# Unread products of TensorE placed by the planner, and weight loads that wait for the one before the last

## The chip, the cores and the metric

The kernel runs on one core of one Trainium2 chip, in one launch. The metric is the device time of one execution in microseconds. The kernel before the change takes 1048.31 us (median of 3 runs, 1048.13 to 1048.65).

## What is computed

Chunked attention with memory keys, followed by two feed-forward layers over the same 3072 tokens:

```python
for c in range(nc):                       # 24 chunks of 32 queries, 16 keys to the left, 8 to the right, 8 memory keys
    scores = scale * np.matmul(q_c, k_full.transpose(0, 1, 3, 2))
    scores = scores - np.max(scores, axis=-1, keepdims=True)
    a = np.exp(scores)
    a = a / (np.sum(a, axis=-1, keepdims=True) + 1e-09)
    out[:, :, c_start:c_end] = np.matmul(a, v_full)
...
x = out.transpose(0, 2, 1, 3).reshape(3072, 512)
h = x @ w_in                              # 512 x 2048
x = (h * np.clip(h + 3.0, 0.0, 6.0) / 6.0) @ w_out
h = x @ w2_in
out = np.maximum(0.01 * h, h) @ w2_out
```

Four batches, 8 heads of 64, 768 tokens each. The four weight matrices come as 64-bit floats.

## The kernel before

Every matrix product of the layers is made of three products of TensorE: an operand is split into a high part that TensorE takes exactly and the low rest (`xh`, `xl`; the two halves of a `w` tile), and high by high, high by low and low by high are added up in PSUM. A weight block (128 by 512) is loaded as 512 KB of 64-bit words into a `w` tile and decoded: absolute value on ACT (line 397), clamp, shift, sign and low bits on DVE (lines 400, 404, 408, 412), then the high part (a cast on ACT, line 342) and the low part (a difference on DVE, line 345). The reference's two layers are worked off in blocks of 512 tokens; later blocks are paired and use seven products in place of eight (line 1327). That part makes up most of the run and is not touched.

The beginning is what the change is about. The first 512 tokens come from two units of attention of 384 tokens (heads 0 to 3 in PSUM pair `at`, heads 4 to 7 in pair `ab`) and two half units (in banks `h` and in pair `ac`). Each goes through the same steps: load of queries and keys, copies of key windows (line 342, on ACT, DVE or POOL), scores on PE (lines 549 and 816), maximum on DVE, exponentials on ACT (lines 573, 585, 842, 850), sum and normalisation on DVE (lines 603, 867), transposes on PE (607, 871), a copy on ACT, product with the values on PE (627, 887), and the split into `xh` (ACT) and `xl` (DVE, line 345). Then come the hidden products `h` of layer 1 (line 1003), the gate on ACT and DVE which gives `g`, and the output products `y` (line 1052).

Nothing of the order is written down by hand. Every step is a `Task` with a key, a cost for each engine that may do it, the steps it comes after, and the buffers that it takes (`allocs`) and uses. `schedule` plays through these with its own costs (among them a model of SP's loads and of the delivery of PE's instructions, `feed`) and issues the steps in the order in which they are picked; each engine then works through its queue in order. The chip waits on semaphores, so the planner's times only set the order.

TensorE is kept at work in the beginning by products whose result nobody reads, the identity by itself into pair `ac`:

```python
x = made(b)[:, 1, N - 128 * c:].rearrange("p (a n) -> p a n", a=c)
for _ in range(n):
    nc.tensor.matmul(x, ident, ident.unsqueeze(1).to_broadcast([128, c, 128]), ...)
```

`warm(n, after)` makes a step of n of them; the four calls after the half units and the loop behind them give their places: 6 of 512 columns and 12 of 256, each tied to a step after which it comes. The last twelve go to the very `ac` in which the second half unit's scores lie. A product of 32-bit numbers is two instructions of TensorE in the profile, so `x4` there is two products here.

SP issues all loads in the planner's order. `LOADS` and `WEIGHTS` are the keys of the first of them. A load waits for a free buffer and for one of eight slots; the first weight loads wait for nothing else.

Of the kernel before, what the change touches and what calls it, by code (L numbers as in the profile page):

```python
# [25 lines left out]
NC = G // CHUNK  # L26
# [31 lines left out]
RATE_QK, RATE, RATE_V, COLD = 380.0, 220.0, 300.0, 1.1  # L58
# [10 lines left out]
class Task:  # L69


    def __init__(self, fn, opts, key, after=(), allocs=(), uses=(), moe=False, issues=1, late=0, loads=False, ins=8):
        self.late, self.loads, self.ins = late, loads, ins
# [21 lines left out]
STARTS, LANDS, SURE = 1900.0, 500.0, 1500.0  # L95
HELD, FETCHED, FETCH, STALL = 447, 256, 5000.0, 250.0
# [7 lines left out]
def schedule(tasks, places, ends):  # L104
# [10 lines left out]
    queue = (0, HELD, None)  # L115

    def feed(at, task):
        used, held, comes = queue
        for _ in range(task.ins):
            if comes is not None and comes <= at:  # L120
                held, comes = held + FETCHED, None
            if comes is None and used >= held - FETCHED:
                comes = at + FETCH
# [35 lines left out]
    def finish(task, e):  # L159
        for b in task.bufs:  # L160
# [6 lines left out]
        for t in task.next:  # L167
# [3 lines left out]
            if not t.left:  # L171
                push(now + (MARGIN if "PE" in t.opts and not t.moe else 0.0), "ready", t)
# [5 lines left out]
    while events:  # L178
# [10 lines left out]
        while again:  # L189
            again = False  # L190
            for e, h in heaps.items():
# [32 lines left out]
                if pick is None:  # L224
                    continue
                pick.taken = True
                for b in pick.allocs:
# [8 lines left out]
                if e == "SP" or pick.loads:  # L236
                    at = now
                    for _ in range(pick.issues):
                        at = max(at, lanes[e].pop(0)) + ISSUE[e]
                        wire = max(wire, at + STARTS) + d / pick.issues  # L240
                        lanes[e].append(wire + LANDS)
                    free[e] = at if pick.loads else max(at, wire - QUEUED)
                    push(free[e], "free", None)
                    push(wire + LANDS + (SURE if pick.allocs else 0.0), "done", (pick, e))
# [12 lines left out]
def tile_attn_moe_moe2(ctx: ExitStack, tc: tile.TileContext, raw, w1i, w1o, w2i, w2o, out):  # L257
# [131 lines left out]
    def decode(src, f, key, early=None, after=(), place="wm", gate=(), late=0, own=True, split=None):  # L389
# [3 lines left out]
        def load(e):  # L393
            nc.sync.dma_start(out=make(t, ([128, 512, 2], U32)).rearrange("p w s -> p (w s)"), in_=src[f])
# [19 lines left out]
        k = add(load, {"SP": dma(524288, 380.0)}, key - 30 if early is None else early, after=after, allocs=[t])  # L414
# [31 lines left out]
    xbuf, xdone, turn, sent = {}, {}, [], {}  # L446

# [9 lines left out]
    marks = {}  # L457

    def warm(n, after=None, home=None):

        b, c = home or Buf("ac"), 2 if home else 4

        def fn(e):
            x = made(b)[:, 1, N - 128 * c:].rearrange("p (a n) -> p a n", a=c)
            for _ in range(n):
                nc.tensor.matmul(x, ident, ident.unsqueeze(1).to_broadcast([128, c, 128]), start=True, stop=True, skip_group_check=True)  # L466

        add(fn, {"PE": c * n * (220.0 if after else 430.0)}, after.key + 0.5 if after else -200.0, after=[after] if after else [], allocs=[] if home else [b], uses=[home] if home else [], ins=4 * n)

    def unit(j, quad, key, tag, own=False, direct=False, loads=None):  # L470
# [254 lines left out]
        t = marks["s", j, quad] = add(scores, {"PE": (COLD if direct else 1.0) * 1300.0}, key - 16, ins=192, after=t, allocs=[ps], uses=[*qk, *kw])  # L725
        scored = t
        if direct and quad in SHIFT:
            t = add(greatest, {"DVE": 2100.0}, key - 15, after=[t], allocs=[mx, e], uses=[ps])
            t = add(exp_all, {"ACT": act(2 * PAIRS * W)}, key - 13, after=[t], uses=[e])
            t = add(total, {"DVE": 1250.0}, key - 12, after=[t], allocs=[s], uses=[e])  # L730
        else:
# [4 lines left out]
            t = add(exp(1), {"ACT": 6 * 330.0}, key - 13, after=[t], uses=[ps, mx, e, s])  # L736
# [3 lines left out]
        t = add(take_p, {"ACT": act(PAIRS * 128)}, key - 5, after=[t], uses=[pt, e])  # L740
        t = marks["v", j, quad] = add(values_whole if plain else values, {"PE": (COLD if direct else 1.0) * 1600.0}, key, ins=192, after=[t, *l2], uses=[e, *v, ps])
# [12 lines left out]
    def half_unit(j, quad, gp, key, tag, loads, copies, cold):  # L754
# [195 lines left out]
        l1 = add(load_qk, {"SP": dma(128 * 2 * QK * 4, RATE_QK)}, loads[0], allocs=[qk])  # L950
# [4 lines left out]
        t = marks["s", j, quad, gp] = add(scores, {"PE": cold * 650.0}, key - 16, ins=96, after=[t], allocs=banks, uses=[qk, kw])  # L955
        marks["b", j, quad, gp] = banks
        if gp or quad not in SHIFT_HALF:
            t = add(greatest, {"DVE": 700.0}, key - 15, after=[t], allocs=[mx], uses=banks)
            t = add(exp, {"ACT": 6 * 330.0}, key - 13, after=[t], allocs=[e, s], uses=[*banks, mx])
            t = add(total, {"DVE": 350.0}, key - 12, after=[t], uses=[s])  # L960
        else:
            t = add(greatest, {"DVE": 1250.0}, key - 15, after=[t], allocs=[mx, e], uses=banks)
# [3 lines left out]
        t = marks["t", j, quad, gp] = add(transpose, {"PE": cold * 300.0}, key - 7, ins=6, after=[t], uses=[e, *banks])  # L966
        t = add(take_p, {"ACT": act(NC * 128)}, key - 5, after=[t], uses=[*banks, e])
        t = marks["v", j, quad, gp] = add(values_whole if whole else values, {"PE": cold * 900.0}, key, ins=96, after=[t, l2], uses=[e, v, *banks])
# [445 lines left out]
    def made_as(b, shape):  # L1414
        return b.t if b.t is not None else make(b, (shape, F32))
# [149 lines left out]
    warm(2)  # L1565
    warm(1, marks["s", 0, 0])
# [124 lines left out]
```

## Time and profile before

| | |
|---|---|
| median of 3 runs | 1048.31 us |
| profiled execution | 1049.14 us |
| its span | 1047.4 us |
| PE busy | 1035.1 us, 99% |
| DVE busy | 875.3 us, 84% |
| ACT busy | 693.7 us, 66% |
| POOL busy | 20.8 us, 2% |
| first hidden product of layer 1 | 39.77 us |

A timeline row gives the start, the time to the end of the last instruction in it, the engine, the line, the tiles and, in brackets, how long the engine had stood idle and what released it. Neighbouring rows overlap a little, as instructions are pipelined. In the stretches the granted clock is a mean: 1.00 is full speed, 0.50 half.

### The profile page before, as it was taken

The numbers are of one execution on the slowest core, as the hardware profiler recorded it, in microseconds if no ns is written. First come the engines' busy times: TensorE is split into PE (matmuls) and PEld (weight loads), VectorE is DVE, ScalarE is ACT, GpSimd is POOL, SyncE is SP. The second block draws the span as 40 slices with busy tenths as digits, with TensorE's granted clock in tenths as the row PEclk, the third lists the DMA queues.
The fourth block names the chain that finished last, engine by engine and source line by source line (L and its number), as shares of the span: only waits on it lengthen the run. The fifth ranks groups of instructions, "written<-read, shape, count | busy, mean of one in ns | idle before, by whom it ended". The sixth has DMA issues, their size and how long they took to land.

```text
span 1047.4 us, 20225 instructions
## 1 busy us (share of the span) xinstructions
PE 1035.1 (99%) x7476; PEld 850.3 (81%) x7476; DVE 875.3 (84%) x1485; ACT 693.7 (66%) x1480; POOL 20.8 (2%) x30
## 2 busy tenths in 40 slices
PE   7999999999999999999999999999999999999998
PEld 4778988888788888888888888888888888888886
DVE  6898988778998778799999899999576998566775
ACT  4786876655888555476686576785565874666753
POOL 3010000000000000000000000000000000000000
PEclk8899999999999999999999999999999999999999
DMA  9889787876887979673648778546342454423451
GB/s 265 283 216 331 241 291 230 258 229 221 262 282 239 332 225 290 239 239 123 214 144 268 253 251 280 183 158 221 111 171 81 174 193 156 173 109 96 146 181 61
DMA packets 127314, 220.49 MB, mean 211 GB/s; under 512 B 12528, under 2 KB 76016, under 8 KB 127216
## 3 DMA queue, kind: packets, MB, share of 16 engines
q1 hardware_dynamic: 127216, 219.20, 63.9%
q8 instruction: 59, 0.97, 0.4%
q14 instruction: 39, 0.32, 0.1%
HBM read 156.24 MB, written 62.91 MB: 209 GB/s over the span
## 4 chain that ended last, share of the span: by engine, by line
PE 89%; DVE 4%; DMA 3%; ACT 3%; issue 1%; SPq 0%; DVEq 0%; ACTq 0%
PE y L1327 15%; PE y L1052 13%; PE y L1495 12%; PE h L1327 10%; PE h L1495 8%; PE hx L1495 8%; PE h L1003 7%; PE hx L1327 7%; PE h L1052 2%; PE at L639 2%; DMA w<-in_raw 2%; PE at L549 1%; DVE w L345 1%; PE at L607 1%; PE ac L466 1%
## 5 line engine op out<-in xcount | busy, mean ns | idle before, releaser
L345 DVE TENSOR_TENSOR w<-w 128x512 fp32r<-128x512 f32 (+2 forms) x393 | 322.9, 854 | 25.8 <-ACT w L342 23.9
L342 ACT CAST w<-w 128x512 fp32r<-128x512 f32 (+1 forms) x290 | 223.3, 803 | 13.4 <-PE hx L1495 3.6
L1052 PE MATMUL y<-g,w 128*128 128x512 f32 (+1 forms) x540 | 125.2, 375 | 0.9 <-ACT g L342 0.7
L1327 PE MATMUL y<-w 128*128 128x512 f32 x516 | 124.6, 390 | 0.0
L1327 PEld LDWEIGHTS y<-w 128*128 128x128 f32 x516 | 96.6, 188 | 20.1
L1052 PEld LDWEIGHTS y<-g,w 128*128 128x128 f32 x540 | 94.1, 189 | 19.0 <-ACT g L342 1.2
L342 ACT CAST g<-w 128x512 fp32r<-128x512 f32 x80 | 49.4, 620 | 63.8 <-PE y L1495 23.0
L1495 PE MATMUL y<-w 128*128 128x512 f32 x384 | 90.3, 389 | 0.0
L1495 PEld LDWEIGHTS y<-w 128*128 128x128 f32 x384 | 72.1, 188 | 14.9
L1301 ACT ACTIVATE w<-w 128x512 f32<-128x512 f32 x72 | 45.0, 630 | 40.4 <-DVE w L1372 18.1
L1003 PE MATMUL h<-xh,w 128*128 128x512 f32 (+1 forms) x288 | 66.1, 370 | 0.5 <-DVE w L345 0.5
L345 DVE TENSOR_TENSOR g<-w,g 128x512 fp32r<-128x512 f32 x80 | 54.1, 684 | 14.3 <-ACT g L342 14.2
L1495 PE MATMUL h<-w 128*128 128x512 f32 x264 | 62.1, 389 | 0.0
L1495 PE MATMUL hx<-w 128*128 128x512 f32 x252 | 59.2, 389 | 0.0
L1327 PE MATMUL h<-xl,w 128*128 128x512 f32 x240 | 58.3, 391 | 0.0
L1495 PEld LDWEIGHTS h<-w 128*128 128x128 f32 x264 | 49.6, 188 | 10.3
L1003 PEld LDWEIGHTS h<-xh,w 128*128 128x128 f32 x288 | 49.7, 189 | 9.9 <-DVE w L345 0.9
L1495 PEld LDWEIGHTS hx<-w 128*128 128x128 f32 x252 | 47.3, 188 | 9.8
L1327 PEld LDWEIGHTS h<-xl,w 128*128 128x128 f32 x240 | 44.8, 188 | 9.9 <-DVE xl L345 0.4
L1327 PE MATMUL y<-xh,w 128*128 128x512 f32 x216 | 52.2, 390 | 0.0
L1327 PEld LDWEIGHTS y<-xh,w 128*128 128x128 f32 x216 | 40.5, 188 | 8.4
L1052 PE MATMUL y<-w 128*128 128x512 f32 x180 | 46.6, 391 | 0.0
(244 smaller groups left out, 1852.2 us busy)
## 6 DMA issues: line engine op xcount, KB each, us to landing
w<-kept2i SPq DMA_DIRECT2D x42, 512.0 KB
w<-kept2o SPq DMA_DIRECT2D x42, 512.0 KB
w<-kept1i SPq DMA_DIRECT2D x28, 512.0 KB
a<-in_raw SPq DMA_DIRECT2D x20, 448.0 KB
w<-in_w1i SPq DMA_DIRECT2D x16, 512.0 KB
w<-in_w1o SPq DMA_DIRECT2D x16, 512.0 KB
w<-in_w2i SPq DMA_DIRECT2D x16, 512.0 KB
w<-in_w2o SPq DMA_DIRECT2D x16, 512.0 KB
```

The lines of the kernel that those rows point to most:

```text
L342: nc.scalar.copy(out, in_) if e == "ACT" else engine(e).tensor_copy(out=out, in_=in_)
L345: engine(e).tensor_tensor(out=out, in0=a, in1=b, op=ALU.subtract)
L466: nc.tensor.matmul(x, ident, ident.unsqueeze(1).to_broadcast([128, c, 128]), start=True, stop=True, skip_group_check=True)
L549: nc.tensor.matmul(ps.t[h * CHUNK:(h + 1) * CHUNK, par, i * W:(i + 1) * W], qk[h // 2].t[r, gp, (h % 2) * G + c * CHUNK:(h % 2) * G + (c + ...
L607: nc.tensor.transpose(pt.t[:, i // NC, (i % NC) * 128:(i % NC + 1) * 128], pview()[:, i * 128:(i + 1) * 128], ident)
L639: nc.tensor.matmul(pv.t[(h % 2) * D:(h % 2 + 1) * D, par, (h // 2) * 2 * G + i * CHUNK:(h // 2) * 2 * G + (i + 1) * CHUNK], v[h // 2].t[r, ...
L1003: nc.tensor.matmul(h.t[:, o:o + n], w.t[:, 1 if p == 1 else 0, k * 128:(k + 1) * 128], x[:, k, c0:c0 + n], start=(p == 0 and k == 0 and o ...
L1052: nc.tensor.matmul(bank(banks[d])[:, c0:c0 + n], w.t[:, 1 if p == 1 else 0, d * 128:(d + 1) * 128], g.t[:, 1 if p == 2 else 0, at:at + n], ...
L1301: return add(lambda e: nc.scalar.activation(out=at(), in_=at(), func=AF.Prelu, alpha=0.01), {"ACT": act(N)}, key, after=[after], uses=uses)
L1327: nc.tensor.matmul(bank(to), wt(l, o)[:, kt * 128:(kt + 1) * 128].bitcast(F32R), operand(p, name, 1 if q == 2 else 0, kt).bitcast(F32R), s ...
L1495: nc.tensor.matmul(bank(to[d]), wt(1 if q == 1 else 0, o)[:, d * 128:(d + 1) * 128].bitcast(F32R), g.t[:, 1 if q == 2 else 0], start=(fres ...
```

## The change

Four things:

1. `warm` and its calls are gone. The planner itself puts in unread products wherever PE would stand idle in its model, as long as no hidden product has been issued. Until the first scores they have 128 columns, later 256. They go into a bank that TensorE itself writes next: `opens` on a step says that from its end on a bank is free for them (the scores have been read), `closes` that a step of PE takes it over.
2. A weight load with index 2 to 23 comes after the landing of the load two before it. POOL copies one element from that tile into the new one (`follow`), and SP's load comes after this copy. All these copies stand in POOL's queue.
3. The planner's figures for the beginning are others: landing of loads, margins, instruction delivery, rates.
4. As the planner orders the whole program, the order of later steps shifts too, on every engine.

```diff
-RATE_QK, RATE, RATE_V, COLD = 380.0, 220.0, 300.0, 1.1
+RATE_QK, RATE, RATE_V, COLD = 380.0, 220.0, 240.0, 1.1
...
-STARTS, LANDS, SURE = 1900.0, 500.0, 1500.0
-HELD, FETCHED, FETCH, STALL = 447, 256, 5000.0, 250.0
+STARTS, LANDS, SURE, SOONER, MOST = 1900.0, 250.0, (0.0, 1500.0), 20000.0, 8000.0
+HELD, FETCHED, ASKS, FETCH, STALL = 447, 256, (256, 400), 2500.0, 250.0
+FIRST, LATER, FIRST_TILL = (128, 430.0), (256, 450.0), 3800.0
...
                 if pick is None:
+                    if e == "PE" and not progress and spots and (begun or now < FIRST_TILL):
+                        cols, took = LATER if begun else FIRST
+                        filler(spots[0], cols)
+                        fill = Task(None, {"PE": took}, 0, ins=4)
+                        end, queue = feed(now, fill)
+                        free[e] = end
+                        push(end, "free", None)
                     continue
...
+        if hold:
+            before, landed = hold
+
+            def follow(e):
+                nc.gpsimd.tensor_copy(out=make(t, ([128, 512, 2], U32))[:1, 0, :1].bitcast(F32), in_=before.t[:1, 0, :1].bitcast(F32))
+
+            k = add(follow, {"POOL": 100.0}, early, after=[*after, landed], allocs=[t], uses=[before])
+            k = add(load, {"SP": dma(524288, 380.0)}, early, after=[k], uses=[t])
...
-    def warm(n, after=None, home=None):
...
+    def filler(b, cols):
+        t = made(b)
+        nc.tensor.matmul((t[:, 1] if b.tag[0] == "a" else t)[:, N - cols:], ident, ident.unsqueeze(1).to_broadcast([128, cols // 128, 128]) if cols > 128 else ident[:, :cols], start=True, stop=True, skip_group_check=True)
...
-        t = marks["t", j, quad] = add(transpose, {"PE": (COLD if direct else 1.0) * 600.0}, key - 7, ins=12, after=[t], uses=[e, ps])
+        t = add(transpose, {"PE": (COLD if direct else 1.0) * 600.0}, key - 7, ins=12, after=[t], uses=[e, ps], closes=[ps])
...
-    warm(2)
-    warm(1, marks["s", 0, 0])
-    warm(2, marks["s", 0, 1])
-    warm(1, marks["s", 1, 0, 0])
-    home = marks["b", 1, 1, 0][0]
-    for m, n in ((("s", 1, 1, 0), 2), (("t", 0, 0), 3), (("t", 0, 1), 3), (("t", 1, 1, 0), 2), (("v", 1, 0, 0), 2)):
-        warm(n, marks[m], home)
...
+            parts = decode(src, f, at - 8, early[i] if i < len(early) else min(at - 38, 6 * i - 40), splits[before:before + 1] if before >= 0 else (), "ys" if i % 2 else ("wm", "st")[f // 2 % 2] if alone_ else "wm", gate=behind if 3 <= i < 6 else (), own=alone_, split=which if alone_ else None, hold=arrivals[i - 2] if 2 <= i < 24 else ())
```

How the order moves, at the three places that the prediction speaks of. Lines of the changed kernel stand 16 to 20 further down: the unread products are 466 before and 488 now, scores 549/569 and 816/836, transposes 607/627 and 871/891, values 627/647 and 887/907, weight loads 394/410.

PE, from the scores of `ac` on, before:

```order
L816 MATMUL ac<-w 32x64 x24
L607 MATMUL at<-ident,w 128x128 x6
L466 MATMUL ac<-ident 128x256 x5
L627 MATMUL at<-w 64x32 x48
L607 MATMUL ab<-ident,w 128x128 x6
L466 MATMUL ac<-ident 128x256 x3
L871 MATMUL h<-ident,w 128x128 x3
L871 MATMUL ac<-ident,w 128x128 x3
L627 MATMUL ab<-w 64x32 x48
```

The same engine in the changed kernel, from the scores of `ab` on:

```order
L569 MATMUL ab<-w 32x64 x48
L627 MATMUL at<-ident,w 128x128 x6
L836 MATMUL h<-w 32x64 x24
L836 MATMUL ac<-w 32x64 x24
L647 MATMUL at<-w 64x32 x48
L488 MATMUL h<-ident 128x256
L891 MATMUL h<-ident,w 128x128 x3
L488 MATMUL h<-ident 128x256 x4
L627 MATMUL ab<-ident,w 128x128 x6
L488 MATMUL h<-ident 128x256 x2
L891 MATMUL ac<-ident,w 128x128 x3
L907 MATMUL h<-w 64x32 x24
```

The transposes and values of `at` stand ahead, the values of `h` ahead of those of `ab`, and 7 unread products are left behind the scores of `ac`, in bank `h`, where 12 in pair `ac` stood. Ahead of these rows stand nine of 128 columns, the scores of `at` and eight of 256 columns.

DVE, around the window copy (four COPY rows) for the second half unit, before (596 is the sum of `at`'s exponentials, 603 its normalisation, 563 to 570 the maximum of `ab`):

```order
L563 MEMSET ab 128x16
L566 TENSOR_REDUCE mx<-ab 128x12
L570 TENSOR_SCALAR mx<-mx 128x12
L596 TENSOR_REDUCE mx<-w 128x12
L598 TENSOR_SCALAR mx<-mx 128x12
L599 RECIPROCAL mx<-mx 128x12
L342 COPY w<-w 128x2x3x56
L342 COPY w<-w 128x2x3x8
L342 COPY w<-w 128x2x3x56
L342 COPY w<-w 128x2x3x8
L603 TENSOR_TENSOR w<-w,mx 128x768
```

In the changed kernel (616, 623, 583 to 590 are the same steps):

```order
L616 TENSOR_REDUCE mx<-w 128x12
L618 TENSOR_SCALAR mx<-mx 128x12
L619 RECIPROCAL mx<-mx 128x12
L623 TENSOR_TENSOR w<-w,mx 128x768
L358 COPY w<-w 128x2x3x56
L358 COPY w<-w 128x2x3x8
L358 COPY w<-w 128x2x3x56
L358 COPY w<-w 128x2x3x8
L583 MEMSET ab 128x16
L586 TENSOR_REDUCE mx<-ab 128x12
L590 TENSOR_SCALAR mx<-mx 128x12
```

The normalisation of `at` has moved ahead of the window copy, the maximum of `ab` behind it.

SP, from the third weight load on, before (774 loads queries and keys of the next half units, 790 and 792 their values):

```order
L394 DMA w<-in_w1i 128x1024
L394 DMA w<-in_w1o 128x1024
L394 DMA w<-in_w1i 128x1024
L394 DMA w<-in_w1o 128x1024
L774 DMA w<-in_raw 128x2x448
L790 DMA w<-in_raw 56x3x128
L792 DMA w<-in_raw 8x3x128
L790 DMA w<-in_raw 56x3x128
L792 DMA w<-in_raw 8x3x128
```

In the changed kernel (410, 794, 810, 812):

```order
L410 DMA w<-in_w1i 128x1024
L410 DMA w<-in_w1o 128x1024
L794 DMA w<-in_raw 128x2x448
L810 DMA w<-in_raw 56x3x128
L812 DMA w<-in_raw 8x3x128
L810 DMA w<-in_raw 56x3x128
L812 DMA w<-in_raw 8x3x128
L810 DMA w<-in_raw 56x3x128
L812 DMA w<-in_raw 8x3x128
L810 DMA w<-in_raw 56x3x128
L812 DMA w<-in_raw 8x3x128
L410 DMA w<-in_w1i 128x1024
```

Two of four weight loads have moved behind the loads of the next half unit, and those behind them follow in pairs.

## Rows read from the trace of the kernel before

**Rows 1.** The page: span; busy time, share and instructions of each engine.
```profile
span 1047.4 us, 20225 instructions
...
PE 1035.1 (99%) x7476; PEld 850.3 (81%) x7476; DVE 875.3 (84%) x1485; ACT 693.7 (66%) x1480; POOL 20.8 (2%) x30
```

**Rows 2.** Timeline of PE to 29 us: start, us, instructions, [idle before <-releaser].
```profile
1.36 3.78 PE L466 MATMUL ac<-ident 128*128 128x512 f32 x4 [1.36 <-POOL three L308]
...
6.28 1.46 PE L549 MATMUL at<-w 64*32 64x64 f32 x92 [0.25 <-DVE w L342]
...
14.37 0.45 PE L816 MATMUL h<-w 64*32 64x64 f32 x29 [1.40 <-issue]
...
18.72 2.93 PE L466 MATMUL ac<-ident 128*128 128x256 f32 x6
23.62 2.08 PE L466 MATMUL ac<-ident 128*128 128x256 f32 x4 [1.97 <-ACT w L850]
25.62 2.97 PE L627 MATMUL at<-w 64*64 64x32 f32 x96
```

**Rows 3.** Timeline of PE from 33 us, same columns.
```profile
33.46 1.78 PE L627 MATMUL ab<-w 64*64 64x32 f32 x96
...
37.14 1.13 PE L466 MATMUL ac<-ident 128*128 128x256 f32 x4
...
39.77 2.17 PE L1003 MATMUL h<-xh,w 128*128 128x512 f32 x8
...
47.28 1.20 PE L1052 MATMUL y<-g,w 128*128 128x512 f32 x4 [0.67 <-ACT g L342]
...
49.27 2.11 PE L1052 MATMUL y<-g,w 128*128 128x512 f32 x8
```

**Rows 4.** Timeline of DVE, same columns.
```profile
15.51 0.77 DVE L342 COPY w<-w 128x336 f32<-128x336 f32 x4 [1.41 <-DMA w<-in_raw]
16.19 0.95 DVE L603 TENSOR_TENSOR w<-w,mx 128x768 f32<-128x768 f32 x1
...
23.60 0.26 DVE L862 TENSOR_SCALAR mx<-mx 128x6 f32<-128x6 f32 x1 [1.62 <-ACT w L850]
...
24.12 0.57 DVE L867 TENSOR_TENSOR w<-w,mx 128x384 f32<-128x384 f32 x1
...
29.72 1.15 DVE L345 TENSOR_TENSOR xl<-at,xh 128x256 fp32r<-128x256 f32 x4 [2.86 <-ACT xh L342]
...
34.75 0.43 DVE L400 TENSOR_SCALAR wm<-wm 128x512 f32<-128x512 f32 x1 [2.07 <-ACT wm L397]
...
48.87 0.68 DVE L345 TENSOR_TENSOR g<-r,g 128x512 fp32r<-128x512 f32 x1
```

**Rows 5.** Timeline of ACT, same columns.
```profile
21.68 0.31 ACT L850 ACTIVATE w<-ac,mx 128x64 f32<-128x64 f32 x1 [2.00 <-PE ac L466]
...
23.14 0.33 ACT L850 ACTIVATE w<-ac,mx 128x64 f32<-128x64 f32 x1
```

**Rows 6.** Stretches: us, busy us (instructions) per engine, granted clock, DMA share, GB/s.
```profile
15.00:20.00 5.00, 4.83 (x59) 3.18 (x59) 4.36 (x17) 2.51 (x11) 1.21 (x2) 0.59 1.07 311
20.00:25.00 5.00, 3.03 (x7) 1.93 (x7) 3.31 (x8) 2.98 (x14) 3.63 (x5) 0.50 0.60 156
25.00:30.00 5.00, 5.00 (x105) 4.31 (x104) 2.14 (x5) 0.99 (x4) 1.18 (x2) 0.50 1.01 397
30.00:35.00 5.00, 5.00 (x107) 4.16 (x107) 2.93 (x8) 2.51 (x5) 0.00 (x0) 0.70 0.57 147
35.00:80.00 45.00, 43.27 (x557) 33.64 (x552) 43.84 (x99) 38.50 (x131) 2.79 (x2) 1.00 0.86 254
```

**Rows 7.** Timeline of SP's DMA queue, same columns.
```profile
24.02 0.43 SPq L394 DMA_DIRECT2D w<-in_w1o  x1
...
72.56 0.41 SPq L394 DMA_DIRECT2D w<-in_w1i  x1
```

**Rows 8.** Timeline of POOL, same columns.
```profile
76.57 1.47 POOL L603 TENSOR_TENSOR w<-w,mx 128x768 f32<-128x768 f32 x1 [5.49 <-ACT w L342]
```

More of the change, by code (lines that the diff above doesn't have):

```diff
@@ L121, in feed @@
                 held, comes = held + FETCHED, None
-            if comes is None and used >= held - FETCHED:
-                comes = at + FETCH
+            if comes is None and used >= held - ASKS[at > 45000]:
+                comes = min(max(at, max((y for x, y in queued if x <= at), default=0.0)) + FETCH, at + MOST)
             if used >= held:
@@ L171, in finish @@
             if not t.left:
-                push(now + (MARGIN if "PE" in t.opts and not t.moe else 0.0), "ready", t)
+                push(now + (MARGIN if "PE" in t.opts and not t.moe and now > SOONER else 0.0), "ready", t)
     for t in tasks:
@@ L387, in tile_attn_moe_moe2, with decode @@
     wbuf, wtask = {}, {}
-    def decode(src, f, key, early=None, after=(), place="wm", gate=(), late=0, own=True, split=None):
+    def decode(src, f, key, early=None, after=(), place="wm", gate=(), late=0, own=True, split=None, hold=()):
         t, m = Buf("w"), Buf(place)
         def load(e):
-            nc.sync.dma_start(out=make(t, ([128, 512, 2], U32)).rearrange("p w s -> p (w s)"), in_=src[f])
+            nc.sync.dma_start(out=made_as(t, [128, 512, 2], U32).rearrange("p w s -> p (w s)"), in_=src[f])
         def absolute(e):
@@ L455, in made @@
         return b.t if b.t is not None else make(b)
-    marks = {}
-    def warm(n, after=None, home=None):
[L461 to L468, printed above, removed]
+    begun_at = Buf("ac")
+    def filler(b, cols):
+        t = made(b)
+        nc.tensor.matmul((t[:, 1] if b.tag[0] == "a" else t)[:, N - cols:], ident, ident.unsqueeze(1).to_broadcast([128, cols // 128, 128]) if cols > 128 else ident[:, :cols], start=True, stop=True, skip_group_check=True)
     def unit(j, quad, key, tag, own=False, direct=False, loads=None):
@@ L965, in half_unit @@
         t = add(norm, {"DVE": 500.0}, key - 11, after=[t], uses=[e, s])
-        t = marks["t", j, quad, gp] = add(transpose, {"PE": cold * 300.0}, key - 7, ins=6, after=[t], uses=[e, *banks])
-        t = add(take_p, {"ACT": act(NC * 128)}, key - 5, after=[t], uses=[*banks, e])
-        t = marks["v", j, quad, gp] = add(values_whole if whole else values, {"PE": cold * 900.0}, key, ins=96, after=[t, l2], uses=[e, v, *banks])
+        t = add(transpose, {"PE": cold * 300.0}, key - 7, ins=6, after=[t], uses=[e, *banks], closes=banks[:1])
+        t = add(take_p, {"ACT": act(NC * 128)}, key - 5, after=[t], uses=[*banks, e], opens=banks[0])
+        t = add(values_whole if whole else values, {"PE": cold * 900.0}, key, ins=96, after=[t, l2], uses=[e, v, *banks], closes=banks)
         jb, at = divmod(begins, N)
@@ L1588, in tile_attn_moe_moe2 @@
             alone_ = f >= KF // 2
-            parts = decode(src, f, at - 8, early[i] if i < len(early) else min(at - 38, 6 * i - 40), splits[before:before + 1] if before >= 0 else (), "ys" if i % 2 else ("wm", "st")[f // 2 % 2] if alone_ else "wm", gate=behind if 3 <= i < 6 else (), own=alone_, split=which if alone_ else None)
+            parts = decode(src, f, at - 8, early[i] if i < len(early) else min(at - 38, 6 * i - 40), splits[before:before + 1] if before >= 0 else (), "ys" if i % 2 else ("wm", "st")[f // 2 % 2] if alone_ else "wm", gate=behind if 3 <= i < 6 else (), own=alone_, split=which if alone_ else None, hold=arrivals[i - 2] if 2 <= i < 24 else ())
             if alone_:
@@ L1639, in tile_attn_moe_moe2 @@
         constants()
-        schedule(tasks, places, ends)
+        schedule(tasks, places, ends, filler, [begun_at])
 def kernel(**inputs):
```

46 lines of the change are left out of this document (28 added, 18 removed).

## The prediction

> **What bounds it now.** I read the page's head first, then the timelines of PE, DVE and ACT up to 50 us, then the stretches, and last SP's queue. TensorE is busy for 99% of the span [rows 1], so nearly all of the time is its own products, which this change leaves alone. What can move is the beginning, where busy does not mean useful: the products of line 466 are read by nobody.
>
> Up to the first hidden layer product at 39.77 [rows 3], PE works through the attention of the first 512 tokens, and its queue is in order. The unread products stand in that queue. Six passes of them run from 18.72, then PE stands 1.97 us until ACT has finished the exponentials of bank pair ac, because the next unread products write into that pair, then four more passes run, and only at 25.62 come the values of unit 0 [rows 2]. The same products had held ACT up: its exponentials on ac wait 2.00 us for line 466 and start at 21.68 [rows 5]. The clock makes it worse: the granted clock is a mean 0.59 in 15 to 20 us, 0.50 until 30 and 0.70 in 30 to 35 [rows 6]. As it has only the two levels 1.00 (2.4 GHz) and 0.50 (1.2 GHz), it fell near 15.9 and rose near 33.0. Before it fell, PE had stood 1.40 us in the middle of the scores of h [rows 2].
>
> DVE is what the beginning leaves unused. It waits 1.41 us for a load before the window copy at 15.51, 1.62 at 23.60, 2.86 for the first xh at 29.72 and 2.07 at 34.75 [rows 4]. From 35 to 80 us it is busy for 43.84 of 45 us, PE for 43.27 [rows 6]: there both are full, and what was not decoded before 35 us is missed later.
>
> **The parts of the change.** The cold pair of wide products, 3.78 us for four passes, 0.945 each [rows 2], becomes nine narrow ones. By columns a pass of 128 takes a quarter, 0.236, so 18 passes take 4.25 us and end near 5.6. The scores of unit 0 now end at 6.28+1.46 = 7.74 with a wait for DVE's window copy inside [rows 2]; a start that is 0.4 later lies beside that wait. I take nothing, at most 0.4.
>
> Eight products of 256 columns now stand between the scores of at and ab. A pass takes 1.13/4 = 0.28 at the full clock [rows 3], so they take 16 x 0.28 = 4.5 us: the scores of ab start at 12.2 and, taking the 1.46 of at's [rows 2], end at 13.7. Instruction delivery could hold them as it holds the scores of h to 14.37 [rows 2], 0.7 us more. Neither is on the path, since DVE comes to ab's maximum only after the window copy that its load holds until 15.51, to 16.3 [rows 4].
>
> In exchange DVE does unit 0 first. Its maximum follows the scores at 7.8; maximum, subtraction and a window copy, exponentials on ACT, sum, reciprocal and the normalisation of 0.95 [rows 4] follow each other and end near 13.4 instead of 17.1. The transposes of at follow ab's scores, the values of at follow the scores of ac (which need the window copy, 16.3), at 17.3 instead of 25.62 [rows 2]. The exponentials of ab now come after those scores and the window copy: 18 exponentials of ab and ac at 0.29 each ((23.14-21.68)/5, [rows 5]) and one batch of h, some 0.5, from 17.5 on ACT end near 23.4, as they do now, when line 466 held them. So ac is normalised near 24.6, as now (24.12+0.57, [rows 4]). The gain starts there: its transposes ran at 33 us in PE's queue, and in the new order only 14 passes of unread products (4 us) and the small steps stand ahead of them, near 26. With the values of h, ab and ac after them (1, 1.8 and 1 us; ab's is 1.78 at the full clock, [rows 3]) the attention ends near 30.2.
>
> From 24.6 I followed the three engines by hand through the new orders. DVE finds xh of at ready, and waits 0.8 and 0.6 us for absolute values on ACT, which stand behind the copies of h, ab and ac, and 0.2 later: 1.6 us in place of 2.86+2.07 = 4.93 [rows 4], so **DVE wins 3.3 us**. On PE the second window copy for `at` on ACT makes it wait again near 30.2; the first hidden products start at 32.5 and end at 38.4. From 24.69 to the second g (48.87+0.68 = 49.55) DVE now needs 24.9 us, of which 4.93 are the two waits: 19.9 for 49 instructions [rows 4]. The new order has 46 up to there, two clamps or shifts (0.34) and one sign step (0.6) fewer: 18.6 us, or 17.3 if each takes no longer than the shortest of its kind, as one clamp took twice its time. With the 1.6 of waits the second g is done between 43.5 and 44.8, values and output products 2.7 later, at 46.2 to 47.5, where they now end at 49.27+2.11 = 51.38 [rows 3]. So **PE is 3.9 to 5.2 us ahead**, 4.6 in the middle, partly because three steps of DVE have moved behind the second g and must be done after it. Both engines are full from 35 to 80 us, so neither count can be had alone: the mean of 3.3 and 4.6 is 3.9. After 80 us the new order holds the same products; what stands ahead stays.
>
> Now the loads. Two of the four that leave SP together up to 24.02 [rows 7] now wait, and with them everything behind them in SP's queue; ahead of w4 and w5 stand one load of queries and keys and eight of values, 0.85 MB, and the landing of w2 and w3. At the 397 GB/s of 25 to 30 us [rows 6] w5 lands between 32 and 35.5; ACT comes to it at 34.6. So it costs 0 to 1; I take 0.3, as most of that stretch lies ahead of ACT. The 22 copies of one element on POOL lie on an engine that is busy 20.8 us in all [rows 1] and are covered by its idle time: nothing. What they can hold up is POOL's queue and with it SP's (rival 4).
>
> On the clock the rows speak against part of this. Between the hidden products (38.4) and the output products (42.2 to 43) PE has only some 1.4 us of work by my count, where now it waits 0.67 for g [rows 3] and keeps 1.00. That is nearer to what went before the fall at 15.9. The Trainium skill (TensorE: Matmul & The Clock Gate, HAM oscillation — how this bites in real kernels) tells of a kernel whose bursts of products are parted by waits, and whose clock is throttled again in every one; by it the sum would be that of the second rival, without it the sum is the one that follows.
>
> **Sum.** 3.9 - 0.3 = 3.6 us off a span of 1047.4 [rows 1]: 1043.8. The profiled execution took 1049.14, 1.74 more than its span, and 0.83 more than the median of the runs, 1048.31. Against the median: **1044.7**.
>
> **The rivals.**
> 1. More is kept (chance 0.18). PE's whole lead of 5.2 or, if the waits before g vanish, the 7.2 us by which the hidden products start sooner (39.77 to 32.5) stays: 1041.1 to 1043.1. For it speaks that PE has 1.73 us of idle in 35 to 80 [rows 6]; against it that DVE has only 1.16.
> 2. The clock falls before the output products (0.17). After the fall at 15.9 PE ran without a gap from 23.62 to 33.0 before the clock rose [rows 2, 6]: 9.4 us, of which half, 4.7, would be lost on dense products; if they bring it back in half that time, 2.4. 1044.7 + 2.4 to 4.7 = 1047.1 to 1049.4, most likely 1047.6. For it: the gap; against it: there are dense products on both sides.
> 3. The loads come too late later on (0.13). By the sizes in SP's order w8 is landed after 12.85 MB instead of 11.53 (the shapes in SP's order added up): 1.32 MB at 254 GB/s [rows 6] is 5 us. If half of it shows as waits of ACT and DVE, 2.5: 1047.2; if less than 1, it is the forecast. Against it: the output of one hidden block takes over 6 us, and weights are decoded a block ahead.
> 4. Slower (0.10): POOL becomes a gate. Its queue is in order, and before the normalisation that now starts at 76.57 [rows 8] stand the copies for loads up to w16, each of which waits for a landing and a free buffer. w16 leaves SP at 72.56 now [rows 7], 4 us ahead of it; in the new order it stands behind 21.63 MB instead of 20.05, 6.2 us later. From the point where the copy comes after 76.57 the normalisation, the transposes and PE behind them wait, and the late step of DVE too, whose in-place write waits for the copy that reads its weight. All of 6.2 us: 1050.9. Against it: the order everywhere is shifted to the front.
>
> **How the numbers follow.** The forecast (within 1.5 us of 1044.7) has 0.42, the rivals 0.18, 0.17, 0.13 and 0.10. About 0.2%, 2.1 us, is what a measurement can tell from no change: 1046.2 and 1050.4 are the bounds. Faster: 0.42 + 0.18 + some 0.06 of rivals 2 and 3 = 0.66; slower 0.10; the same 0.24. The range leaves out the best tenth and the worst: 1041.2 to 1048.3.
>
> **What would show it.** Right: values of at near 17 us, no wait of ACT for an unread product, first hidden product between 31 and 34, the first output products done near 46, DVE idle by 3 us less before 35. Wrong: a granted clock below 1.00 after 40 us (rival 2), waits of ACT or DVE for w loads between 40 and 70 (rival 3), POOL waiting on a load ahead of a normalisation (rival 4), or a first hidden product near 39, which would mean that I read PE's order wrongly.

## The result and the profile after

The changed kernel takes **1059.91 us** (median of 6 runs, 1054.08 to 1062.88), the kernel before 1048.3 in the runs beside it: a ratio of 1.0103, 95% interval 1.0087 to 1.012, so 11.6 us slower. The forecast of 1044.7 us was wrong in its sign, and the range 1041.2 to 1048.3 doesn't hold the result.

The head of the page, which answers to [rows 1]:

```profile
span 1059.2 us, 20331 instructions
...
PE 1033.6 (98%) x7488; PEld 853.7 (81%) x7488; DVE 875.9 (83%) x1486; ACT 694.3 (66%) x1477; POOL 30.0 (3%) x54
```

PE is busy 1.5 us less in a span that is 11.8 us longer. The time went into waits of PE. The timeline of PE in the changed kernel (columns as in [rows 2]):

```profile
17.84 0.56 PE L647 MATMUL at<-w 64*64 64x32 f32 x19
19.68 1.50 PE L647 MATMUL at<-w 64*64 64x32 f32 x77 [1.28 <-issue]
...
31.86 1.56 PE L907 MATMUL ac<-w 64*64 64x32 f32 x42 [1.56 <-issue]
...
34.25 3.78 PE L1022 MATMUL h<-xh,w 128*128 128x512 f32 x8
...
44.11 1.14 PE L919 MATMUL at<-w 64*64 64x32 f32 x48 [1.86 <-ACT w L358]
45.17 4.60 PE L1071 MATMUL y<-g,w 128*128 128x512 f32 x12
...
68.02 1.19 PE L1071 MATMUL y<-g,w 128*128 128x512 f32 x4 [0.92 <-ACT w L358]
72.11 3.48 PE L1071 MATMUL y<-g,w 128*128 128x512 f32 x8 [2.90 <-POOL w L361]
...
79.84 3.07 PE L1071 MATMUL y<-g,w 128*128 128x512 f32 x12 [1.28 <-ACT w L358]
...
118.56 1.10 PE L1022 MATMUL h<-xh,w 128*128 128x256 f32 x7 [3.07 <-issue]
```

Up to 35 us it went nearly as forecast. The values of `at` come at 17.84 (in two pieces; before at 25.62 [rows 2]) and the first hidden products at 34.25, 5.5 us ahead of 39.77 [rows 3]. Then the lead is lost and more. The first eight hidden products take 3.78 us, where they took 2.17 before [rows 3]: 1.6 us of the lead go there. PE waits for a copy on ACT ahead of 44.11, for decoded weights ahead of the output products at 68.02, 72.11 and 79.84, and for nothing that the profile shows ahead of 118.56.

Stretches of the kernel before, beyond [rows 6] (columns as there):

```profile
80.00:130.00 50.00, 49.86 (x852) 45.04 (x851) 45.42 (x92) 38.41 (x130) 1.48 (x1) 1.00 0.84 280
130.00:300.00 170.00, 169.62 (x1834) 138.54 (x1834) 141.44 (x265) 115.05 (x313) 2.95 (x2) 1.00 0.80 256
```

The same stretches of the changed kernel, with two short ones ahead:

```profile
40.00:45.00 5.00, 3.14 (x59) 2.53 (x58) 3.84 (x7) 3.04 (x7) 0.57 (x2) 1.00 0.93 336
45.00:50.00 5.00, 5.00 (x60) 3.79 (x53) 4.01 (x9) 4.17 (x13) 0.00 (x0) 0.66 1.08 286
...
35.00:80.00 45.00, 38.04 (x367) 29.27 (x366) 37.19 (x81) 32.05 (x105) 7.14 (x14) 0.89 0.96 282
80.00:130.00 50.00, 45.86 (x646) 41.19 (x646) 40.09 (x79) 34.75 (x109) 3.16 (x7) 1.00 0.65 207
130.00:300.00 170.00, 166.40 (x1915) 135.55 (x1914) 140.75 (x270) 110.61 (x319) 6.68 (x4) 1.00 0.79 254
```

The balance can be read from the first PE number and the clock. From 35 to 300 us PE is idle 6.96 + 4.14 + 3.60 = 14.70 us, before 1.73 + 0.14 + 0.38 = 2.25: **12.4 us more**. The granted clock of 0.89 in 35 to 80 takes up to 0.11 x 45 = **5.0 us** of products. The beginning is **5.5 us** ahead. 12.4 + 5.0 - 5.5 = 11.9; the spans differ by 11.8, so nothing is left for the time after 300 us. The 6.96 us are the four waits of the timeline from 44.11 to 79.84, and the 4.14 are the 3.07 ahead of 118.56 and one more of 1.07 for nothing that the profile shows.

Where do the waits of 68 to 80 us come from? SP's weight loads in the kernel before, the eighth to the fourteenth after the first:

```profile
41.28 0.36 SPq L394 DMA_DIRECT2D w<-in_w1i  x1
...
42.21 0.37 SPq L394 DMA_DIRECT2D w<-in_w1i  x1
...
51.01 0.36 SPq L394 DMA_DIRECT2D w<-in_w1o  x1
58.01 0.40 SPq L394 DMA_DIRECT2D w<-in_w1i  x1
58.50 0.38 SPq L394 DMA_DIRECT2D w<-in_w1o  x1
```

And in the changed kernel:

```profile
45.35 0.36 SPq L410 DMA_DIRECT2D w<-in_w1i  x1
...
52.03 0.35 SPq L410 DMA_DIRECT2D w<-in_w1i  x1
...
59.55 0.35 SPq L410 DMA_DIRECT2D w<-in_w1i  x1
64.39 0.35 SPq L410 DMA_DIRECT2D w<-in_w1o  x1
67.07 0.35 SPq L410 DMA_DIRECT2D w<-in_w1i  x1
```

Count for count each leaves SP 4 to 10 us later, while PE began 5.5 us earlier. The last four stand in another order; the same load compared with itself, the seven leave 3.3 to 15.4 us later. And ACT, which never waits for one of these loads in the kernel before, waits 8.4 us for them in the changed kernel (us in total, times, longest):

```profile
ACT wm L413 <- DMA w<-in_w1i: 6.7, 3, 3.4
...
ACT ys L413 <- DMA w<-in_w1o: 1.7, 1, 1.7
```

The chain of waits of the changed kernel follows one of them (start, us, what):

```profile
64.39 5.75 DMA w<-in_w1o
...
70.29 0.17 POOL w L434
...
70.77 1.30 POOL w L361
...
72.11 3.48 PE y L1071 x8
```

The load from 64.39 lands at 70.14; POOL's one-element copy for the load after next waits for it, and behind that copy in POOL's queue stands the low part (line 361) that PE's output products need. After this wait the eight products take 3.48 us; the eight at 49.27 before took 2.11 [rows 3].

### The profile page after: what moved, and what is told of

Read it like the earlier page. It is cut to its first block, busy times and chain, and to the rows that moved or that the text cites. A ratio compares the mean times of both kernels' runs of the same rounds, so it can differ in the third digit from the quotient of the medians.

```text
span 1059.2 us, 20331 instructions
## 1 busy us (share of the span) xinstructions
PE 1033.6 (98%) x7488; PEld 853.7 (81%) x7488; DVE 875.9 (83%) x1486; ACT 694.3 (66%) x1477; POOL 30.0 (3%) x54
## 4 chain that ended last, share of the span: by engine, by line
PE 89%; DMA 5%; DVE 2%; ACT 2%; issue 1%; SPq 0%; POOLq 0%; POOL 0%; ACTq 0%; DVEq 0%
PE y L1346 16%; PE y L1071 12%; PE y L1514 12%; PE h L1346 11%; PE h L1514 8%; PE hx L1346 8%; PE hx L1514 8%; PE h L1022 7%; DMA w<-in_raw 2%; PE h L1071 2%; PE at L659 2%; PE at L569 1%; PE at L627 1%; DMA attended<-a 1%; DMA w<-in_w1i 1%
## 5 line engine op out<-in xcount | busy, mean ns | idle before, releaser
L1071 PE MATMUL y<-g,w 128*128 128x512 f32 (+1 forms) x540 | 127.6, 381 | 6.2 <-POOL w L361 2.9
L358 ACT CAST g<-w 128x512 fp32r<-128x512 f32 x80 | 49.8, 623 | 68.7 <-PE y L1514 22.3
L1022 PE MATMUL h<-xh,w 128*128 128x512 f32 (+1 forms) x288 | 69.4, 380 | 3.1 <-issue 3.1
```

Of the source, the lines that this page charges most:

```text
L358: nc.scalar.copy(out, in_) if e == "ACT" else engine(e).tensor_copy(out=out, in_=in_)
L1022: nc.tensor.matmul(h.t[:, o:o + n], w.t[:, 1 if p == 1 else 0, k * 128:(k + 1) * 128], x[:, k, c0:c0 + n], start=(p == 0 and k == 0 and o ...
L1071: nc.tensor.matmul(bank(banks[d])[:, c0:c0 + n], w.t[:, 1 if p == 1 else 0, d * 128:(d + 1) * 128], g.t[:, 1 if p == 2 else 0, at:at + n], ...
```

## The experiments

Times are medians, ratios are to the kernel before in the runs beside it, with the 95% interval. Three questions were asked: what do the copies and holds cost, what is the beginning worth, and what does it cost by itself that the planner deals the whole order again.

**The copies alone, in the order of before.** Every engine keeps the rows of before, and POOL gets the copy that ties a load to the one before the last:

```diff
         def load(e):
-            nc.sync.dma_start(out=make(t, ([128, 512, 2], U32)).rearrange("p w s -> p (w s)"), in_=src[f])
+            make(t, ([128, 512, 2], U32))
+            if 2 <= len(arrivals) < 24:
+                nc.gpsimd.tensor_copy(out=t.t[:1, 0, :1].bitcast(F32), in_=arrivals[-2].t[:1, 0, :1].bitcast(F32))
+            arrivals.append(t)
+            nc.sync.dma_start(out=t.t.rearrange("p w s -> p (w s)"), in_=src[f])
```

> The order of the kernel before to the row on PE, DVE, ACT and SP; the 22 copies on POOL are issued ahead of weight loads 2 to 23, so that a load waits for the landing of the one two before it. Theory A (held loads come too late): slower by 3 us or more, with waits of ACT for weight loads between 40 and 90 us. Theory R: the holds cost under 2 us by themselves.

1053.23 us (4 runs), ratio 1.0047 [1.003, 1.0063]. The 22 copies that I costed at nothing cost some 5 us. POOL's timeline in this kernel:

```profile
81.55 0.17 POOL L396 COPY w<-w 1x1 f32<-1x1 f32 x1 [4.86 <-DMA w<-in_w1i]
81.69 1.46 POOL L607 TENSOR_TENSOR w<-w,mx 128x768 f32<-128x768 f32 x1
```

PE's timeline in it:

```profile
83.20 0.88 PE L611 MATMUL at<-ident,w 128*128 128x128 f32 x6 [3.51 <-POOL w L607]
...
92.79 1.17 PE L553 MATMUL at<-w 64*32 64x64 f32 x96
```

And one of its stretches:

```profile
84.00:88.00 4.00, 4.00 (x51) 2.83 (x51) 2.30 (x6) 3.19 (x5) 0.29 (x1) 0.57 0.94 355
```

The normalisation that started at 76.57 [rows 8] starts at 81.69, right behind a copy that waited for a landing. PE, which ran the same transposes at 79.68 before, runs them at 83.20, 3.5 us later, and then the granted clock is a mean 0.57 for 4 us; the scores at 92.79 stood at 87.66 before, 5.1 us. So half of the wait is paid a second time: 3.5 + 1.6.

Two parts of these copies, by the bounds of the loads alone (`2 <= len(arrivals) < 12`, and `12 <= len(arrivals) < 24`):

> The kernel before, its order kept on every engine; one-element copies on POOL only ahead of the weight loads 2 to 11. Theory A (what costs is the normalisation that stands behind late copies in POOL's queue): none of these copies can be late at 76.57 us, so the time is that of before within 0.2%, 1046 to 1049 us, and the normalisation starts at 76.5 to 77. Theory B (loads that are kept apart from the start come late for ACT and DVE): about half or more of the 5 us that all 22 copies cost, 1050 to 1053 us, with PE behind by 2 us or more at 80 us.

> The kernel before, its order kept; copies only ahead of the weight loads 12 to 23, seven of them ahead of the normalisation on POOL. Theory A: most of the 5 us of all 22 copies is here, 1050.5 to 1053.5 us, the normalisation starts 2 to 5 us later than 76.57, and PE waits for it at the transposes of at by 2 to 4 us. Theory B: under half of it, 1047 to 1050 us.

1051.12 us (12 runs), ratio 1.0032 [1.0019, 1.0045], and 1051.82 us (10 runs), 1.0033 [1.0019, 1.0046]. Neither theory has it alone. With the early copies the last copy is done at 53 us, long before the normalisation, but a weight is late: ACT waits 2.83 us for it, PE then 2.53. ACT and PE, from two timelines of the kernel with the copies for loads 2 to 11:

```profile
64.11 0.66 ACT L401 ACTIVATE ys<-w 128x512 f32<-128x512 f32 x1 [2.83 <-DMA w<-in_w1o]
```

```profile
70.03 4.61 PE L1056 MATMUL y<-g,w 128*128 128x512 f32 x12 [2.53 <-ACT w L342]
```

With the late copies it is POOL's queue again. POOL and PE in that kernel:

```profile
78.65 0.17 POOL L396 COPY w<-w 1x1 f32<-1x1 f32 x1 [5.08 <-DMA w<-in_w1i]
78.86 1.47 POOL L607 TENSOR_TENSOR w<-w,mx 128x768 f32<-128x768 f32 x1
```

```profile
80.38 1.54 PE L611 MATMUL at<-ident,w 128*128 128x128 f32 x6 [4.38 <-POOL w L607]
```

PE came to these transposes at 76.0, 3.7 us ahead of 79.68 before, and the lead bought only a longer wait; the granted clock then was 0.50 from 80 to 86. By the ratios each half costs 3.4 us, and there are two mechanisms, a late weight and POOL's queue.

**The holds in an order that is dealt again.** The changed kernel's order, each row of PE, DVE, ACT and SP, without its copies; then with the copies for loads 2 to 11 only:

```diff
-                nc.gpsimd.tensor_copy(out=make(t, ([128, 512, 2], U32))[:1, 0, :1].bitcast(F32), in_=before.t[:1, 0, :1].bitcast(F32))
+                make(t, ([128, 512, 2], U32))
```

> The changed kernel's order on PE, DVE, ACT and SP to the row; only the 22 copies on POOL are not issued, so that a weight load waits for a buffer and a slot alone. Theory A (loads held by the landing of the one two before): the thirteenth weight load leaves SP well before 55 us (59.55 with the copies), ACT's 8.4 us of waits for weight loads and PE's 2.9 us wait for POOL go, and the time is 1045 to 1051. Theory B (delivery of PE's instructions, 10 us of waits named issue): these waits stay near 10 us and the time stays above 1055. Theory C (the new order itself is bad): as B, with the waits at other places.

> The changed kernel, its order kept on every engine; the copies ahead of the weight loads 12 to 23 are not issued, those for 2 to 11 are. Theory A: as good as without any copies, 1054 to 1057 us, and PE's wait for the low part on POOL near 72 us is gone. Theory B: as slow as the changed kernel, 1058 to 1061 us.

1055.58 us (5 runs), 1.0092 [1.0048, 1.0137], and 1057.78 us (6 runs), 1.0101 [1.008, 1.0121]. Both intervals overlap that of the changed kernel, so **the copies themselves are not shown to cost anything in its own order**. That order is late without them. Two of SP's weight loads in the kernel without copies, which left at 58.50 (`in_w1o`) and 58.01 (`in_w1i`) before:

```profile
64.48 0.35 SPq L410 DMA_DIRECT2D w<-in_w1o  x1
66.15 0.35 SPq L410 DMA_DIRECT2D w<-in_w1i  x1
```

PE in it:

```profile
78.76 4.62 PE L1071 MATMUL y<-g,w 128*128 128x512 f32 x12 [5.01 <-ACT w L358]
```

In SP's queue the loads of values stand right ahead of them, from 62.06 to 64.38 here and from 61.76 to 64.29 in the changed kernel, so these weights leave about as late without a copy; that the loads of values are what holds them was not tested. PE's wait for the low part on POOL falls from 2.90 to 0.25 us (0.18 with the early copies), and the next output products wait 5.01 for a decoded weight instead of 1.28. The chain of waits that ends there runs through the load of 64.48 again; its decoding on ACT then stands behind 12 exponentials. So most of the lateness comes back at another place. The 12 products behind it take 4.62 us, those before took 2.9.

No hold at all (`hold=()`), and holds for loads 2 to 7 only, both planned again; then the kernel before with the holds added:

```diff
-hold=arrivals[i - 2] if 2 <= i < 24 else ())
+hold=())
```

> The changed kernel with hold=() for all weight loads, so that the planner orders without them; the unread products and the planner's figures stay as changed. Theory A: 1044 to 1048, the gain of the beginning (some 4 us) is kept. Theory B: 1053 or more, with issue waits of some 8 us. Theory C, if the planner's new figures are at fault: 1053 or more, without issue waits.

```diff
-hold=arrivals[i - 2] if 2 <= i < 24 else ())
+hold=arrivals[i - 2] if 2 <= i < 8 else ())
```

> Only weight loads 2 to 7 are held, which are the ones that share the wires with the attention's loads of the first block. Theory A with the loss in the later holds (from 40 us on): 1044 to 1050. If the early holds do the harm: near the changed kernel's 1060.

```diff
-        k = add(load, {"SP": dma(524288, 380.0)}, key - 30 if early is None else early, after=after, allocs=[t])
+        if hold:
...
+            k = add(follow, {"POOL": 100.0}, early, after=[*after, landed], allocs=[t], uses=[before])
+            k = add(load, {"SP": dma(524288, 380.0)}, early, after=[k], uses=[t])
```

> The kernel before with the holds alone (its unread products and its planner's figures as they were). Theory A: slower than before by 5 to 12 us. Theories B and C: within 3 us of before.

1052.2 us (10 runs), 1.0043 [1.0025, 1.0061]; 1052.88 us (9 runs), 1.0046 [1.003, 1.0063]; 1056.17 us (5 runs), 1.0084 [1.0056, 1.0111]. By the ratios, taking the holds out of the changed kernel gives back 0.60 of its 1.03%, some 6 us, and adding them to the kernel before costs 0.84%. So the larger part seems to be what the planner makes of the holds: its order puts the weight loads further back. Each of these is an order dealt again, though, and two null changes (below) lie 0.56% apart: 0.84% is clear of that, 0.60% hardly. Holds for loads 2 to 7 alone add nothing to having none (1.0046 and 1.0043), so what holds cost seems to come with those from load 8 on. The other 0.43% needs no hold.

**The beginning alone.** The last twelve unread products of before are not issued, and every other row of every engine stays:

```diff
         def fn(e):
+            if home:
+                return
```

> The order of the kernel before to the row on every engine, with its last twelve unread products left out when the program is written (the planner still counts them). Theory R (any newly planned order loses what this one order had won; the change of the beginning itself is good or neutral): faster than before or the same, 1043 to 1049. Theory D (the unread products cover the delivery of instructions and hold the clock): 1049 to 1055, with issue waits in the values and a clock at 0.50 after 35 us.

1048.47 us (10 runs), 1.0008 [0.9992, 1.0023]: no change. Its timeline of PE:

```profile
33.57 0.63 PE L889 MATMUL ac<-w 64*64 64x32 f32 x7 [4.56 <-issue]
...
35.42 3.76 PE L1005 MATMUL h<-xh,w 128*128 128x512 f32 x8
...
66.32 3.02 PE L1054 MATMUL y<-g,w 128*128 128x512 f32 x12 [1.02 <-ACT w L342]
```

SP in the same kernel:

```profile
53.52 0.36 SPq L394 DMA_DIRECT2D w<-in_w1o  x1
60.38 0.40 SPq L394 DMA_DIRECT2D w<-in_w1i  x1
```

The hidden products start 4.4 us ahead, the output products that stood at 68.42 still 2.1, and the span (1046.7) ends 0.7 shorter. The order is the same, so nothing but time was lost. 1.6 us went at once, as the first eight products ran at half clock after PE's wait (3.76 us, 2.17 before [rows 3]). From 45 to 62 us the lead stays at 3.2. Another 1.6 went in waits for decoded weights, 1.02 ahead of 66.32 and 0.33 and 0.27 up to 74, for the loads leave SP 2.5 and 2.4 us **later** than the 51.01 and 58.01 of before, though PE is ahead. This is the plainest sign that around 70 us the loads and their decoding set the pace, and not when PE begins.

The unread products by other steps, each planned again: none of the last twelve in the kernel before; all but three of them; the planned ones with the old figures and no holds; the new figures with the old ones and no holds.

```diff
-    for m, n in ((("s", 1, 1, 0), 2), (("t", 0, 0), 3), (("t", 0, 1), 3), (("t", 1, 1, 0), 2), (("v", 1, 0, 0), 2)):
+    for m, n in ():
```

> The kernel before without its last twelve unread products (the ones into pair ac after 17 us); no holds, the planner's figures as before. Theory D (the unread products cover time in which PE would wait for the delivery of its instructions, and keep the clock): PE shows waits named issue of 2 us or more in the values of h, ab or ac and the clock is at 0.50 for longer than the 17 us of before; the first hidden product starts only some 3 us sooner and the time is 1047 to 1053. Theory of the prediction (they only stand in the way): first hidden product near 33 us, 1042 to 1045.

```diff
-    for m, n in ((("s", 1, 1, 0), 2), (("t", 0, 0), 3), (("t", 0, 1), 3), (("t", 1, 1, 0), 2), (("v", 1, 0, 0), 2)):
+    for m, n in ((("s", 1, 1, 0), 2), (("t", 0, 1), 3), (("t", 1, 1, 0), 2), (("v", 1, 0, 0), 2)):
```

> The kernel before with three unread products fewer, those after at's transposes; nothing else. Theory D: the values of at start near 21 us instead of 25.6, but within 0.2% of before in all (1045 to 1049), as the next block of instructions or DVE ends the wait. Theory of the prediction: 3 us or more faster.

```diff
-STARTS, LANDS, SURE, SOONER, MOST = 1900.0, 250.0, (0.0, 1500.0), 20000.0, 8000.0
-HELD, FETCHED, ASKS, FETCH, STALL = 447, 256, (256, 400), 2500.0, 250.0
+STARTS, LANDS, SURE, SOONER, MOST = 1900.0, 500.0, (1500.0, 1500.0), 0.0, 8000.0
+HELD, FETCHED, ASKS, FETCH, STALL = 447, 256, (256, 256), 5000.0, 250.0
```

> The planned unread products with the planner's old figures and no holds. If they make the loss that stays without holds: 1050 to 1054, with issue waits of 4 us or more before 35 us and a clock below 1.00 between 35 and 55 us. If the figures make it: 1045 to 1049.

```diff
-                    if e == "PE" and not progress and spots and (begun or now < FIRST_TILL):
+                    if False:
...
+    warm(2)
+    warm(1, marks["s", 0, 0])
```

> The planner's new figures with the unread products placed by hand as before and no holds. If the figures make the loss that stays without holds (some 5 us): 1051 to 1054. If the planned unread products make it (delivery of instructions and the clock): 1045 to 1049.

1054.32 us (4 runs), 1.0069 [1.0042, 1.0096]; 1057.5 (4), 1.0094 [1.0072, 1.0115]; 1054.48 (4), 1.0065 [1.0042, 1.0089]; 1051.64 (10), 1.0033 [1.002, 1.0047]. All four are slower, also the one that only takes three products away. No one part of the change explains this. In two of them a part of the loss is waits of PE for nothing that the profile shows, 4.6 us in four with three fewer, and without the last twelve (us in total, times, longest):

```profile
PE ac L887 <- issue: 3.7, 1, 3.7
```

**Dealing the order again.** So the planner was given two null changes: one figure moved by 2%, and another by 0.7%. The first leaves the first 83 rows of PE as they were, the second 92.

```diff
-STARTS, LANDS, SURE = 1900.0, 500.0, 1500.0
+STARTS, LANDS, SURE = 1900.0, 510.0, 1500.0
```

> The kernel before with one figure of the planner moved by next to nothing (the landing of a load 510 in place of 500 ns); PE's order is the same for its first 83 rows, some 115 us, and differs here and there up to mid-run. Theory R: slower by 2 to 10 us though nothing in the beginning changed, with new waits of PE between 115 and 400 us. Theories A and D: within 1.5 us of before.

```diff
-STARTS, LANDS, SURE = 1900.0, 500.0, 1500.0
+STARTS, LANDS, SURE = 1900.0, 500.0, 1490.0
```

> The same with another figure (the margin behind a load's landing 1490 in place of 1500 ns); PE's order is the same for its first 92 rows, some 130 us. Theory R: slower by 2 to 10 us, not by the same amount or at the same places as with the other figure. Theories A and D: within 1.5 us of before.

1046.4 us (10 runs), 0.9982 [0.9973, 0.9992], and 1051.86 us (10 runs), 1.0038 [1.0021, 1.0054]. Two changes that mean nothing move the time by -0.2% and +0.4%. Of seven orders dealt again without holds (the five above that have none, and these two) one is faster than before and six are slower by 3.6 to 9.4 us, and the mean of their ratios is 1.0046. Five of them carry a part of the change, so this isn't the price of dealing alone; but with two null changes this far apart, none of their differences of 3 or 4 us can be put down to the part that it carries.

The one at 510 also shows the lead going without a low clock: its beginning ran at 1.00, the hidden products start at 35.44, 4.3 us ahead, and then PE waits 1.6 us in three for decoded weights and 1.8 in two for normalisations.

This order without the last twelve unread products:

```diff
-STARTS, LANDS, SURE = 1900.0, 500.0, 1500.0
+STARTS, LANDS, SURE = 1900.0, 510.0, 1500.0
...
+            if home:
+                return
```

> The kernel before with the planner's landing time of loads at 510 in place of 500 (the order of e11), and the last twelve unread products are not issued. If the lead of the beginning is only worth something where later waits do not take it, PE is 4 to 6 us ahead at 40 us and the end is within 1 us of e11's 1046.4: 1045.4 to 1047.4 us. If the lead adds up with e11's order, 1 us or more below e11: 1043.5 to 1045.4 us.

1047.08 us (12 runs), 0.9986 [0.9976, 0.9997]. Its interval lies below 1, as that of the one at 510 does; leaving the products out adds nothing to it. Both are 0.1 to 0.2% off, at the edge of what can be told.

## Why the prediction was wrong

**What held.** The beginning came as I had followed it: values of `at` at 17.84 against 17.3, first hidden products at 34.25 against 32.5 and within 31 to 34 but for 0.3, unread products that no longer wait for ACT, and of DVE's waits of 2.86 and 2.07 us [rows 4] one of 1.43 is left. The first output products are done at 49.8, 1.6 us before 51.4 but not at 46.2 to 47.5: here the clock comes in, below.

**"After 80 us the new order holds the same products; what stands ahead stays."** This step failed, and with it the term of 3.9 us. The same sentence treats two things as given. The first is that a lead is kept: in the order of before, a lead of 4.4 us at 35 us was 2.1 at 66 and 0.7 at the end, and the weights left SP 2.4 us later all the same. Nor was the whole lead of 5.5 us there to be won: in two executions with the same rows of PE at a clock of 1.00 the hidden products start 4.0 to 4.3 us ahead of the one that I read, without this change (last section). I had seen that DVE and PE are both full from 35 to 80 us and took the mean of both counts; the third partner, SP's queue with its landings, was left out of the mean. The second is that the same products in another order take the same time. Null changes alone moved it by 0.6% from end to end. The rows could have warned me: PE is idle for only 1.73 us in 35 to 80 [rows 6], and in the seven orders dealt again without holds it is idle for 2.9 to 5.4 there.

**"So it costs 0 to 1; I take 0.3."** Mis-sized. I priced the delay of w4 and w5 only. In rival 3 I worked out 5 us for w8 from the sizes in SP's queue, measured 4.1 and up to 10 for later loads, and put what PE and the others would pay at half. ACT's waits for loads came to 8.4 us, and PE paid 0.92, 2.90 and 1.28 us for decoded weights between 67 and 80, and the clock on top. What I held against it, that weights are decoded a block ahead, failed: the lead that PE still had (1.6 us at 49.8) and the loads' delay of 4 to 10 us together use up a block of over 6.

**"The 22 copies ... nothing."** Rival 4 named the place, the price and the way: in the order of before the normalisation moved from 76.57 to 81.69 behind the copies and PE waited 3.5 us. I gave it 0.10. In the changed kernel the step held up was the low part at 70.77 and not the normalisation, and that copies cost anything there beyond the late loads isn't shown.

**The clock.** Rival 2 came true beside the others: the granted clock was a mean 0.66 in 45 to 50 us, after a stretch in which PE was busy for 3.14 of 5, and the twelve output products took 4.60 us, where twelve took 2.9 later: 1.7. I had put it at 2.4 to 4.7 and at one place. In fact it was low before that, a mean 0.65 in 30 to 35 and 0.67 in 35 to 40, behind the wait of 1.56 ahead of 31.86, and it fell again after the wait of 2.90 (0.57 from 72 to 76 us), and in the experiments after waits of 2.53, 3.51, 4.38 and 5.01. It stayed at 1.00 after 0.92 and 1.28, and also after the 3.07 ahead of 118.56, so the length of a wait alone doesn't decide. The output products behind such waits cost 1.4 us (3.48 for 2.11) to 1.7 (4.60 and 4.62 for 2.9) more. The Trainium skill (TensorE: Matmul & The Clock Gate, HAM oscillation — how this bites in real kernels) tells of this loss being paid again in every burst of products behind a wait. That agrees with the rows behind the waits of 1.56 to 5.01 us named first, and not with those behind the 3.07.

**PE's instructions.** My price of 0.7 us for instruction delivery was one wait. The waits of PE without a releaser add up to 10.0 us in the changed kernel (us in total, times, longest):

```profile
PE h L1022 <- issue: 3.1, 1, 3.1
...
PE ab L569 <- issue: 2.1, 1, 2.1
PE at L569 <- issue: 2.0, 2, 1.1
```

The other two are the 1.56 and 1.28 of the timeline above. Before there was one of 1.40 [rows 2]. 4.1 us of these (the 3.07 and the 1.07 ahead of 95.85) are all the idle time that PE has from 80 to 130 us, and 0.91 follows at 135.57. Counted in matmuls and weight loads of the trace, the six stand behind 449, 705, 1218, 2497, 3266 and 3777 instructions: 449 plus multiples of 256, to within one. So do all such waits of over 0.6 us in the other runs, 450 in the kernel before and 1217 in the one with the 4.56 among them. So they belong to fixed places in PE's stream and not to what stands there, as waits for the next block of instructions would. That the delivery alone makes them isn't shown, as no run changed it by itself.

**Open.** Which of the planner's figures makes the holds so dear in SP's order was not tried, nor whether the changed kernel with SP's order of before would keep its lead.

## What to carry to other kernels

Where several queues are near full, a lead of one engine is worth only as much as the slowest of the others, loads included, also comes earlier: follow each weight from its place in the load queue to its product before a gain is booked. A copy that only orders two loads puts its wait into its engine's in-order queue, so look for the next real work behind it. And where a planner deals the whole order again, measure a null change of it first: its spread (here -0.2% to +0.4% from only two) is the least that a real gain must beat.

## What was not expected of the hardware

With the same rows of PE in the beginning the granted clock was 0.50 from 20 to 30 us in the kernel before [rows 6], and in the kernel with the late copies 1.00, as here:

```profile
25.00:30.00 5.00, 4.69 (x115) 4.16 (x115) 4.93 (x12) 4.15 (x10) 0.69 (x2) 1.00 1.00 394
```

The hidden products started at 35.79 there and at 39.77 before; in the kernel with 510, at 1.00 from 15 to 35, they started at 35.44. Of the 85 executions of the kernel before that ran beside the experiments, 77 show a mean granted clock of 0.995 or more over the whole span, the profiled one 0.992. So what one profile shows of the beginning holds for that execution, and part of my argument rested on a low clock that another execution of the same rows doesn't have: against 35.44 and 35.79 the changed kernel's 34.25 is a lead of 1.2 to 1.5 us, not 5.5.
